# A decode kernel with more kept V, slots given out while the plan is made, and PSUM banks shared out differently

## The chip, the cores and the metric

The kernel runs on one core of a Trainium2 chip. The metric is the device time of one execution in microseconds; the median of several executions is quoted. The engines are PE (TensorE, the matrix engine, with its weight loads listed apart as PEld), DVE (VectorE), ACT (ScalarE), POOL (GpSimd) and SP, which here only issues transfers. SBUF is the on-chip memory with 128 partitions, PSUM the memory into which PE writes its sums; this kernel divides it into eight banks. "The stream" below is the flow of K and V from the chip's memory into SBUF.

## The reference

Two kinds of layer alternate, A, B, A, B, for eight rows of one token each:

```python
def _A_ref(x, k_cache, v_cache, wq, wo):          # 16 query heads, 8 KV heads, 4096 keys of 256
    q = ... x @ wq ...
    scores = jnp.einsum("bhqd,bhkd->bhqk", q, k) * (Dh ** -0.5)
    p = _softmax(scores, axis=-1)
    o = jnp.einsum("bhqk,bhkd->bhqd", p, v)
    return o... @ wo
def _B_ref(x, w1, w2, w3, w4): ...                # per token; with one token it is an MLP, w3 and w4
x = x + _A_ref(_layernorm(x), K, V, wq, wo)       # layer one
x = x + _B_ref(_layernorm(x), ...)
x = x + _A_ref(_layernorm(x), K, V, wq, wo)       # layer two: the same K and V
x = x + _B_ref(_layernorm(x), ...)
```

K and V of one row and head are 2 MB each. Both attention layers read the same caches, so what of a row stays in SBUF between its two layers need not be read again.

## The kernel before

Python code makes a list of operations with their dependencies, a scheduler orders them on each engine by modelled durations, and the engines get fixed instruction streams with semaphore waits. SBUF holds 30 slots for "quarters" (a quarter of one head's K or V, 128 partitions x 4096 bytes, 0.524 MB). Of each row, five K heads (20 quarters) and two V quarters are kept from layer one to layer two; 8 slots then carry the stream.

```python
KEEP_K = 5
KEEP_V = 2
...
def grab(n):                      # at program-building time, before anything is scheduled
    rank = {q: k for k, q in enumerate(free_slots)}
    for k, margin in ((4, MARGIN4), (2, MARGIN2), (1, 0)):
        ...                       # a run of 4, 2 or 1 slots, those freed longest ago first
...
# front(): K of a head. transposes of K pieces, then scores into the one score bank
wr=[("sc", par, x) ...], banks=["S"]
plan.op("dve", lambda v: v.tensor_reduce(pm, sview, ...), ..., banks=["S"])   # max, from PSUM
plan.op("act", ex, ..., banks=["S"])                                          # two exps, from PSUM
...
# back(): V of a head. weighted sum into the one bank psP, two evictions, row sums
par, no = 0, g % NO
ps, bk = psP, "P"
last = t.matmul(ps[g4:g4 + 2, PV0:PV0 + DH], pT[nr][:, i, :], slot_ap(q, s * 256, 256), ...)
plan.op("dve", lambda v: v.tensor_copy(oS[:, 0, :], po), ...)
plan.op("dve", lambda v: v.tensor_tensor(oS[:, 1, :], po, oS[:, 0, :], ALU.subtract), ...)
...
bank, bk2 = ROWS[layer]           # one bank for the row sums of each layer, four row groups
last = t.matmul(bank[32 * i:32 * i + 1, 0:D], oT[no][...], wo_sb[:, a:a + D], ...)
```

While row b's MLP (a chain of small operations, with the stream's kept slots occupied) runs between its two layers, the V of three heads of row b+1 keeps the stream busy. The last row, 7, has no next row; there an MLP over the other seven rows is done too.

## Time and profile before

| | before |
|---|---|
| median of 3 executions | 1143.41 us (1142.17 to 1145.31) |
| profiled span | 1139.0 us |
| loads | 455.19 MB in 376 cache loads and the weights |
| load queue, share of 16 engines' span | 97.3% |
| PE, PEld, DVE | 85%, 68%, 48% |
| granted PE clock | 0.932 |

How to read it: the transfers are busy nearly always, so the bytes set the time. The list of issues tells how they are cut (lines of the first page: tensor, count, KB of each, median us from issue to landing):

```profile
kv<-in_A_v_cache_dram SPq DMA_DIRECT2D x57, 2048.0 KB, 16.5
kv<-in_A_k_cache_dram SPq DMA_DIRECT2D x55, 2048.0 KB, 23.4
...
kv<-in_A_v_cache_dram SPq DMA_DIRECT2D x128, 512.0 KB, 11.3
```

A quarter takes 1.24 us at 424 GB/s, so the 11.3 us from issue to landing are at most nine quarters' worth, less what a load needs to start flowing (about 2 us, by the prediction's estimate): seven or eight quarters were in the queue when it was issued. That fits 8 slots all in flight at the MLPs: the slots, not the issue, seem to bound how far ahead the stream can be.

### The profile page before, as it was taken

The page shows a single profiled execution, that of the slowest core. Times are in us where ns is not written, and L with a number is a line of the kernel's source. Part 1 is how long each engine was busy: PE and PEld are TensorE (multiplying, and loading weights), DVE is VectorE, ACT ScalarE, POOL GpSimd, SP SyncE. Part 2 cuts the span into 40 slices and gives each one's busy share as a digit, 9 for nine tenths or more (in the row PEclk, how much of TensorE's full clock was granted, in tenths as well). Part 3 has the DMA queues.
Part 4 walks back from the last instruction along what each step waited for, and adds up shares of the span by engine and source line. Part 5 has one row for each costly group of instructions (what it writes and reads, how often), then busy time and mean ns, then how long its engine had stood idle before and what let it go on. Part 6 is the DMA issues. An engine that isn't in the chain of part 4 may idle for free.

```text
span 1139.0 us, 42316 instructions
## 1 busy us (share of the span) xinstructions
PE 967.5 (85%) x19513; PEld 775.8 (68%) x19513; DVE 541.1 (48%) x1630; ACT 259.8 (23%) x826; POOL 97.6 (9%) x273
## 2 busy tenths in 40 slices
PE   5788888898789987998888987989868998898887
PEld 4677566685668756886667855777557875676675
DVE  3344434554255543565445643555425554354453
ACT  1133112340123301232022410233012330232120
POOL 0000010010100100010010100011010010010010
PEclk9999899998899988899999988999899899999897
DMA  9999999999999999999999999999999999999992
GB/s 334 408 423 394 411 409 424 421 415 376 422 423 420 415 385 424 425 417 413 399 423 424 414 408 399 423 421 417 386 422 424 419 414 398 424 416 412 361 410 108
DMA packets 58705, 457.89 MB, mean 402 GB/s; under 512 B 6288, under 2 KB 9504, under 8 KB 26400
## 3 DMA queue, kind: packets, MB, share of 16 engines
q1 hardware_dynamic: 58528, 455.19, 97.3%
q8 instruction: 153, 2.51, 0.9%
q14 instruction: 24, 0.20, 0.0%
HBM read 455.16 MB, written 0.01 MB: 400 GB/s over the span
## 4 chain that ended last, share of the span: by engine, by line
DMA 45%; PE 43%; DVE 4%; issue 4%; SPq 3%; ACT 0%; POOL 0%
DMA kv<-in_A_k_cache_dram 23%; DMA kv<-in_A_v_cache_dram 22%; PE psT L985 14%; PE psS L836 12%; PE psP L887 7%; SPq L480 3%; PE psT L1153 2%; PE psM L692 2%; PE psR L934 2%; PE psM L789 1%; DVE oS L901 1%; DVE oS L899 1%; PE psM L708 1%; PE psM L792 1%; PE psP L909 1%
## 5 line engine op out<-in xcount | busy, mean ns | idle before, releaser
L985 PE MATMUL psT<-ident_f,kv 128*128 128x128 f32 x2816 | 389.5, 289 | 36.8 <-DMA kv<-in_A_k_cache_dram 31.9
L985 PEld LDWEIGHTS psT<-ident_f,kv 128*128 128x128 f32 x2816 | 322.8, 147 | 66.9 <-DMA kv<-in_A_k_cache_dram 42.6
L993 DVE COPY kv<-psT 128x512 f32<-128x512 f32 x401 | 273.9, 691 | 189.3 <-PE psT L985 181.8
L994 ACT COPY kv<-psT 128x512 f32<-128x512 f32 x303 | 177.8, 587 | 405.3 <-PE psT L985 401.1
L887 PE MATMUL psP<-kv,pT 128*2 128x256 bf16 x4096 | 164.4, 286 | 32.3 <-DMA kv<-in_A_v_cache_dram 18.6
L857 ACT ACTIVATE pT<-psS,nb 128x32 bf16<-128x32 f32 x256 | 75.3, 300 | 351.8 <-DVE nb L851 351.8
L836 PE MATMUL psS<-q2T,kv 128*128 128x48 bf16 x4096 | 134.2, 187 | 20.4 <-issue 18.3
L836 PEld LDWEIGHTS psS<-q2T,kv 128*128 128x128 bf16 x4096 | 122.4, 99 | 37.7 <-issue 32.2
L887 PEld LDWEIGHTS psP<-kv,pT 128*2 128x2 bf16 x4096 | 81.9, 84 | 72.4 <-issue 27.6
L836 PEld LDWEIGHTS psS<-q1T,kv 128*128 128x128 bf16 x4096 | 123.0, 97 | 9.7 <-issue 5.3
L836 PE MATMUL psS<-q1T,kv 128*128 128x48 bf16 x4096 | 128.9, 184 | 0.0
L849 POOL PARTITION_ALL_REDUCE gm<-pm x128 | 45.4, 355 | 775.5 <-DVE pm L847 775.5
L847 DVE TENSOR_REDUCE pm<-psS 128x2 f32<-128x64 f32 x128 | 28.7, 224 | 148.5 <-PE psS L836 146.5
L899 DVE CAST oS<-psP 128x256 bf16<-128x256 f32 x128 | 54.2, 423 | 63.5 <-PE psP L887 59.7
L1153 PE MATMUL psT<-ident_b 128*128 128x512 bf16 x220 | 75.3, 426 | 0.0
L862 POOL PARTITION_ALL_REDUCE Db<-rs x128 | 51.0, 398 | 229.5 <-ACT pT L857 229.5
L909 PEld LDWEIGHTS psP<-sel,oS 128*128 128x128 bf16 x512 | 25.7, 100 | 62.2 <-DVE oS L901 59.6
L909 PE MATMUL psP<-sel,oS 128*128 128x2 bf16 x512 | 32.2, 167 | 37.3 <-DVE oS L901 36.6
L901 DVE TENSOR_TENSOR oS<-psP,oS 128x256 bf16<-128x256 f32 x128 | 54.2, 424 | 3.2
L857 ACT ACTIVATION_READ_ACCUMULATOR pT<-psS,nb 128x1 f32 x256 | 50.9, 199 | 0.0
L934 PE MATMUL psR<-wo_sb,oT 128*1 128x448 bf16 x448 | 42.5, 368 | 6.2 <-DVE oT L915 3.0
L692 PE MATMUL psM<-x2c,wq_sb 128*128 128x24 bf16 x768 | 36.9, 184 | 9.0 <-issue 7.1
(121 smaller groups left out, 475.8 us busy)
## 6 DMA issues: line engine op xcount, KB each, us to landing
kv<-in_A_v_cache_dram SPq DMA_DIRECT2D x57, 2048.0 KB, 16.5
kv<-in_A_k_cache_dram SPq DMA_DIRECT2D x55, 2048.0 KB, 23.4
kv<-in_A_v_cache_dram SPq DMA_DIRECT2D x70, 1024.0 KB, 14.0
kv<-in_A_k_cache_dram SPq DMA_DIRECT2D x66, 1024.0 KB, 20.1
kv<-in_A_v_cache_dram SPq DMA_DIRECT2D x128, 512.0 KB, 11.3
wo_sb<-in_A_wo_dram SPq DMA_DIRECT2D x1, 3584.0 KB, 46.4
wq_sb<-in_A_wq_dram SPq DMA_DIRECT2D x3, 1024.0 KB, 17.0
w_sb<-in_B_w_dram SPq DMA_DIRECT2D x3, 448.0 KB, 22.8
```

The costliest lines, as they stand in the source:

```text
L692: last = t.matmul(bank[:, at + i * step:at + i * step + copies], w, r, start=(kc == 0), stop=(kc == 3))
L836: last = t.matmul(ps[:, 2 * i:2 * i + 2 * REP], a[:, c:256:2], bcast(rhs(c), REP, 1), start=(c == 0), stop=(c == 1))
L857: return a.activation(pT[nr][:, :, :].rearrange("p i j -> p j i")[:, jj, :], sview[:, jj, :], ACT.Exp, bias=nb[nm][:, jj:jj + 1], scale=IN ...
L887: last = t.matmul(ps[g4:g4 + 2, PV0:PV0 + DH], pT[nr][:, i, :], slot_ap(q, s * 256, 256), start=(i < 4), stop=(i >= 28), skip_group_check= ...
L899: plan.op("dve", lambda v: v.tensor_copy(oS[:, 0, :], po), 0.36, "o", rd=[("pv", par, x) for x in range(4)], wr=["oS0"], banks=[bk], prio=hi)
L901: plan.op("dve", lambda v: v.tensor_tensor(oS[:, 1, :], po, oS[:, 0, :], ALU.subtract), 0.36, "o", rd=["oS0"] + [("pv", par, x) for x in r ...
L909: last = t.matmul(ps[:, PV1 + 2 * c:PV1 + 2 * c + 2], oS[:, w, c:DH:2], sel[:, :], start=(w == 0), stop=(w == 1))
L934: last = t.matmul(bank[32 * i:32 * i + 1, 0:D], oT[no][:, i % 2, i // 2:i // 2 + 1], wo_sb[:, a:a + D], start=(k == 1), stop=(k == HKV - 1 ...
L985: last = t.transpose(psT[bank][:, s * P:(s + 1) * P], src, ident_f[:, :])
L993: return e.tensor_copy(dst, psT[bank][:, :])
L994: return e.copy(dst, psT[bank][:, :])
L1153: return t.matmul(psT[bank][:, :], ident_b[:, :], bcast(ident_b[:, :], 4, 1), start=True, stop=True)
```

## The change

Its intent: keep one V quarter more, and make seven working slots do what eight did. Slots are no longer fixed in program order but given out by the scheduler when its own clock says that a load could start, in runs of one to four. PSUM's eight banks are shared out anew: two banks for weighted sums (used in turn), paid for by putting both layers' row sums into one bank. The scores are copied to SBUF at once, so the score bank is free earlier. In the last row all queries come first and the seven-row MLP comes after three tasks.

The diff below leaves out smaller edits: the softmax has two sets of buffers in place of three, the scheduler counts 3.5 us from the issue of a load to its start in place of 2.4, and layer two's heads run as one list in place of two. The two MARGIN constants stand in the diff, but nothing in the changed kernel reads them.

```diff
-KEEP_V = 2
-MARGIN4, MARGIN2 = 16, 8
+KEEP_V = 3
+MARGIN4, MARGIN2 = 6, 2
+MLP_AT = 3
 ...
+    def next_kv(i):                       # in the scheduler, at each step
+        m = ...                           # up to 4 neighbouring quarters of one head, same fate
+        late = max(free["sp"], dma_end - self.LEAD)
+        ...                               # first time at which m neighbouring slots are free,
+        ...                               # or, if that is later than `late`, a shorter run
+        return t, m, q
 ...
-    psP = nc.alloc_psum_tensor("psP", [P, 512], f32)
-    psR = [nc.alloc_psum_tensor(f"psR{i}", [P, 512], f32) for i in range(2)]
+    psP = [nc.alloc_psum_tensor(f"psP{i}", [P, 512], f32) for i in range(2)]
+    psR = nc.alloc_psum_tensor("psR", [P, 512], f32)
 ...
+        plan.op("dve", lambda v: v.tensor_copy(ss[:, :], ps[:, 0:64]), 0.17, "max", rd=scs,
+                wr=[("sS", nm)], banks=[bk], prio=hi)      # max and exps then read ss
 ...
-        par, no = 0, g % NO
-        ps, bk = psP, "P"
+        par = g % 2
+        ps, bk = psP[par], f"P{par}"
 ...
-                    last = t.matmul(bank[32 * i:32 * i + 1, 0:D], ...
+                    r = 64 * layer + 32 * (i % 2)
+                    last = t.matmul(psR[r:r + 1, 0:D], ...   # two row groups a layer, not four
 ...
+            k = both(1, b, l2_heads, [(1, b, h) for h in free_heads])   # last row
+            run(k[:MLP_AT])
             mlp(x3T[:, :, :], "x3all", B, xoT[:, :, :], ["xo"])         # was after all of k
```

## The prediction

> **What bounds the kernel now.** I read the first page from the top: totals, the 40 slices, the queue and its issues.
>
> ```profile
> span 1139.0 us, 42316 instructions
> PE 967.5 (85%) x19513; PEld 775.8 (68%) x19513; DVE 541.1 (48%) x1630; ACT 259.8 (23%) x826; POOL 97.6 (9%) x273
> ...
> DMA  9999999999999999999999999999999999999992
> GB/s 334 408 423 394 411 409 424 421 415 376 422 423 420 415 385 424 425 417 413 399 423 424 414 408 399 423 421 417 386 422 424 419 414 398 424 416 412 361 410 108
> ...
> q1 hardware_dynamic: 58528, 455.19, 97.3%
> ```
>
> The transfers are at nine tenths or more in 39 of 40 slices, and the load queue's packets fill 97.3% of sixteen engines' span. PE at 85% looks close, but this count contains 220 filler matmuls (75.3 us) whose only purpose is the clock, and pipelined matmuls overlap in it. So the kernel is bound by the stream of K and V, and I ask only three things: how many bytes, in what packets, and where the stream stops.
>
> The stream's full rate comes from cutting the run into stretches. First a stretch of 2 MB loads (16 KB packets), then one of 512 KB loads (4 KB packets), then the stretch of the single-row MLP between layers, in pieces of 2 us:
>
> ```profile
> 200.00:220.00 20.00, 16.93 (x285) 14.37 (x284) 9.91 (x23) 5.79 (x17) 1.51 (x4) 1.00 1.01 426
> 258.00:264.00 6.00, 4.36 (x83) 2.52 (x81) 2.22 (x8) 1.43 (x6) 0.75 (x2) 1.00 1.02 412
> ...
> 276.00:278.00 2.00, 2.00 (x70) 1.93 (x67) 0.00 (x0) 0.00 (x0) 0.00 (x0) 0.96 0.97 385
> 278.00:280.00 2.00, 2.00 (x40) 1.23 (x42) 0.56 (x3) 0.00 (x0) 0.00 (x0) 0.50 0.53 211
> 280.00:282.00 2.00, 1.93 (x35) 0.91 (x23) 1.45 (x8) 0.00 (x0) 0.00 (x0) 0.69 0.91 236
> ```
>
> The last column is GB/s. 426 with 16 KB packets, 412 with 4 KB packets, and a dip to 211 while the MLP runs. Doing the same for every microsecond of the run, and counting what each microsecond below 340 GB/s lost against 424, gives this budget: start 5.4 us; seven MLP dips near 143, 272-282, 413, 548, 683, 819 and 954 us, 9.2 us together; one at 99 us, 0.9; 1059 to 1083 us, 3.9; the end from 1117 us, 21.2.
>
> Why the dip? The timeline of VectorE and PE there:
>
> ```profile
> 272.96 0.61 PE L887 MATMUL psP<-kv,pT 128*2 128x256 bf16 x16
> ...
> 274.19 0.41 DVE L899 CAST oS<-psP 128x256 bf16<-128x256 f32 x1
> 274.63 0.42 DVE L901 TENSOR_TENSOR oS<-psP,oS 128x256 bf16<-128x256 f32 x1
> ...
> 278.32 1.02 PE L887 MATMUL psP<-kv,pT 128*2 128x256 bf16 x16
> ```
>
> A head's weighted sum ends at 273.5 us, its eviction waits behind the MLP's small VectorE operations until 274.19, and the next head's first matmul into the same bank comes only at 278.32. For almost 5 us no V slot comes free, and the queue runs dry.
>
> The end, from the chain that ended last:
>
> ```profile
> 1115.55 1.81 PE psP L887 x27
> ...
> 1120.21 1.32 PE psP L887 x29
> 1121.55 0.43 DVE oS L899
> ...
> 1123.36 0.90 PE psP L887 x32
> 1124.29 0.44 DVE oS L899
> ...
> 1127.80 0.43 DVE oS L901
> ```
>
> The last bytes land near 1118 us (344 GB/s in 1115-1118, 35 in the next 3 us). By then PE has just left the seven-row MLP (its second matmul block starts at 1113) and still owes several heads, each waiting for the one bank. The last eviction starts at 1127.43; from there to the end is 11.6 us of serial work.
>
> **What the Trainium skill says.** (1) "DMA: Bandwidth & Descriptors", section Specifications: a fabric ceiling of 435 GB/s, and about 358 GB/s from HBM for one core. The trace agrees with the first and not the second: 426 is held for 20 us, so there is no faster rate left to gain and bytes are time. (2) "Perfetto Trace Analysis", section Identifying the Most-Contended Engine: matmul busy share is no measure of nearness to the limit, and the weight-load share is better; here 68% against DMA 97.3%, which agrees with my choice. (3) The same page, Matmuls: independent groups should rotate through PSUM banks, so that an eviction overlaps the next group. The 5 us hole above is what it looks like when they do not. (4) "PSUM — Partial Sum Buffer", section The four PSUM rules: a start flag clears accumulation state over the bank and the 32-partition quadrants written. The two layers' row sums go to rows 0 and 32, and 64 and 96, so they may share a bank; no run so far shows it.
>
> **The change part by part.**
>
> *Third kept V quarter.* A quarter is 128 partitions x 4096 bytes = 0.524 MB. One more kept for each of 8 rows saves 8 x 0.524 = 4.19 MB of 455.19; at 424 GB/s that is **-9.9 us**, all of it on the path. The built instruction stream confirms it: 488 V quarters issued in place of 496, K unchanged at 352.
>
> *Runs of one to four, given out by the plan's clock.* The cache loads go from 376 to 389: 121 of 2 MB (before 112), 22 of 1.5 MB (none), 44 of 1 MB (136), 202 of 512 KB (128). Each load is 128 packets, so 13 x 128 = 1664 packets more. The two rates give the price of a packet: on one engine 16 KB take 16384/(426/16) = 615 ns, four of 4 KB 4 x 4096/(412/16) = 636 ns, so three extra packets cost 21 ns, 7 ns each. 1664 x 7 / 16 engines = **+0.7 us**. The stretches that are full already cannot get fuller by a better choice of slot.
>
> *Two banks for the weighted sums against one slot less.* At an MLP, 20 K quarters and 2 V quarters are held, and 8 slots of 30 carry the stream; after, 7. One slot is 0.524/424 = 1.24 us of stream. What hides the MLP is 12 V quarters of three heads plus the free slots: before 20 x 1.24 = 24.7 us, after 19 x 1.24 = 23.5 us. The need: from the last V of the layer (265.3 us) to the first freed K slots (284.3 to 286.4, when the first scores end) is 19 to 21 us, plus about 2 us from issue to flow (my estimate: the first loads are issued from 0.73 us on, and the first 4 us move 104 GB/s on average, 1 us' worth of full stream, so it flows from 3 us): 21 to 23 us. So 7 slots are just enough if V is used promptly, which the second bank allows. I take a third of the 9.2 us back: **-3 us**, with room either way.
>
> *Copy of the scores out of PSUM.* 128 copies of 128x64, at about the 0.22 us of the reduction over the same elements = 28 us more VectorE, from 48% to about 50%. It lies beside the stream. It frees the score bank some 2 us earlier per head (now held until the second exponential), useful right after an MLP. **0 us** taken by itself.
>
> *One bank for both layers' row sums, a memset and constants.* It pays for the second bank. Same 448 matmuls; row sums now go one after another into two row groups instead of four. 368 ns x 4 per head is all there is, beside the stream. **0 us.**
>
> *The order.* The head order of layer two stays (kept K first). The first load after a kept-K stretch now comes one task earlier. For the last row all queries are made at once and the seven-row MLP is put after three tasks, not after all of them. This takes it off PE's end. In the built order the last heads' weighted sums alternate banks with nothing but filler and row sums between, so PE should be waiting for DMA there. Then the end is one last quarter's 8 matmuls (0.3), eviction to finish 11.6 us as above, and up to 1.3 us for the row-sum evictions that share VectorE: 13 to 14 us after the last byte in place of 20.8. **-6.5 us.** Of the 3.9 us lost at 1059-1083 I take back **0.5**.
>
> Sum: -9.9 + 0.7 - 3 - 6.5 - 0.5 = -19.2 us; 1143.4 - 19.2 = 1124.2. I round up to **1125**, since two of the terms are hopes and the first is arithmetic.
>
> **The rivals.**
> (A) *Bytes saved, holes widened.* The load queue already waits most for scores, and each MLP has one slot less. If each of seven dips loses the full 1.24 us more, and the banks bring nothing, 8.7 us are given back, and with the end gained the time is 1143.4 - 9.9 + 0.7 + 8.7 - 7 = 1136. For it:
>
> ```profile
> SPq L480 <- PE psS L836: 533.2, 96, 20.1
> SPq L480 <- PE psP L887: 315.7, 140, 9.4
> ```
>
> These are slot waits, though, with the queue mostly still full behind them; by themselves they show no loss. Against it: the seen hole is a V hole, not a K one.
> (B) *Everything lines up.* All dips closed and the end at 13 us: 1143.4 - 9.9 + 0.7 - 9.2 - 7.8 - 3 = 1114. Against it: seven slots leave under 1.5 us of slack by my own count.
> (C) *The plan's clock is wrong.* Slots are now chosen by simulated times; where the chip is later, a load waits at the head of the in-order queue for one slot while another stands empty. Or the fewer fillers (166 against 220) leave PE at a lower clock (granted 0.932 on average now). Either could cost several us across the run and end near 1140.
>
> **Range and chances.** Bytes and packets (-9.2) are nearly sure: 1134 with nothing else. The end's -6.5 is likely, the dips may go -9 to +9. Hence 1125, 8 in 10 between 1114 and 1137. Faster by over 2% means below 1120.5, a gain of 22.9: it needs most of the dips closed too, 0.29. Slower by 2% needs a new stall of over 30 us, 0.02. Within 2%: 0.69.
>
> **What would show it.** The queue should move 451.0 MB in about 60,200 packets. Stretches of 2 MB loads should still read 426. Seven dips of under 1 us each confirm the banks; dips of 2.5 us confirm (A), with the queue waiting for scores. From the last byte to the end should be 13 to 14 us. The weighted sum of the next head should start before the eviction of the last one is over. The prediction is wrong if the end stays near 20 us (then PE, not the order, set it), if the full-rate stretches fall below 420, or if new holes appear outside the MLPs, which would be (C).

## The result and the profile after

The changed kernel took 1132.31 us (median of 4, 1130.72 to 1132.89); the kernel before 1144.36 (4 runs in all, 1142.17 to 1147.04). The ratio is 0.9891, 95% interval 0.9867 to 0.9916. A ratio here and below is the mean time of one kernel's runs over that of the other's of the same rounds, so not quite the ratio of the medians. Executions over 1.5% slower than the fastest of the same kernel are left out of the means. It is a real gain of 1.1%, inside the range, and within 2%.

The lines of the first page that answer to those of before:

```profile
span 1131.1 us, 42368 instructions
PE 971.4 (86%) x19459; PEld 776.7 (69%) x19459; DVE 552.0 (49%) x1742; ACT 279.8 (25%) x846; POOL 98.0 (9%) x273
...
GB/s 331 409 424 420 391 414 424 423 413 384 418 424 426 414 381 420 426 423 412 380 426 423 424 400 400 423 424 421 372 413 424 423 418 384 424 422 393 378 376 121
...
q1 hardware_dynamic: 60400, 450.99, 97.7%
...
kv<-in_A_v_cache_dram SPq DMA_DIRECT2D x183, 512.0 KB, 8.7
```

The bytes fell by the 4.2 MB that were kept; the packets rose; the full slices still read 424 to 426. The 512 KB loads now land 8.7 us after their issue. That would fit a shorter queue, but they are no longer the same loads (183 in place of 128), so it is not shown. The slices with the six MLPs between 200 and 1010 us (384, 381, 380, 400, 372, 384) are no better than before (376, 385, 399, 399, 386, 398), and those ahead of the last one read 393, 378, 376 where before they read 412, 361, 410.

There is an exact account of this. Cut the run into microseconds and count for each what it is short of 424 GB/s; then the span is the moved bytes at 424 plus the sum of these losses. Before: 457.89/0.424 + 59.1 = 1139.0. After: 453.70/0.424 + 61.0 = 1131.1. So between these two executions the bytes gave **-9.9 us**, and everything else together **+1.9 us**. They are single executions, and that of the kernel before was a quick one (1140.88 us against a median of 1144.36). By the times of all runs (the mean of two ratios, below) the change gained 12.2 us, 2.3 more than its bytes. So everything else was worth somewhere between 2 us lost and 2 us gained, where the prediction had summed 9.3 us gained. This is where its missing 7 us are.

Did the second bank do what it was for? The timeline of PE and DVE at the same MLP of the changed kernel, with idle time and its releaser in brackets:

```profile
270.28 0.61 PE L970 MATMUL psP<-kv,pT 128*2 128x256 bf16 x16
...
271.48 0.42 DVE L982 CAST oS<-psP 128x256 bf16<-128x256 f32 x1
271.93 0.42 DVE L984 TENSOR_TENSOR oS<-psP,oS 128x256 bf16<-128x256 f32 x1
...
271.88 0.61 PE L970 MATMUL psP<-kv,pT 128*2 128x256 bf16 x16 [0.66 <-DMA kv<-in_A_v_cache_dram]
...
277.89 0.39 PE L970 MATMUL psP<-kv,pT 128*2 128x256 bf16 x8 [0.89 <-DMA kv<-in_A_v_cache_dram]
```

The next head's sum starts at 271.88, while the eviction of the last one is still going on, so that step was right. But where PE waits now, it is for V that has not landed. The hole was not closed, it changed hands. The stretches of 2 us there, last column GB/s:

```profile
270.00:272.00 2.00, 1.34 (x39) 0.74 (x39) 1.83 (x11) 0.00 (x0) 0.00 (x0) 1.00 0.92 332
272.00:274.00 2.00, 2.00 (x44) 0.95 (x37) 0.68 (x4) 0.21 (x1) 0.00 (x0) 1.00 0.90 322
...
278.00:280.00 2.00, 1.75 (x39) 0.87 (x33) 0.91 (x7) 0.00 (x0) 0.00 (x0) 0.93 0.95 315
280.00:282.00 2.00, 2.00 (x17) 0.51 (x14) 1.24 (x5) 0.00 (x0) 0.00 (x0) 0.50 0.95 313
```

One deep dip (211, 236) became two shallow ones of about the same area. Over the whole stretch from 200 to 1010 us, with six MLPs, the loss was 20.4 us before and 22.0 after. Not all of this is in the dips: microseconds under 340 GB/s, the prediction's own measure of a dip, lost 8.4 us of it before and 8.9 after.

The end, in stretches of 3 us (us, PE, PEld, DVE, ACT, POOL busy with counts, clock, DMA share, GB/s):

```profile
1089.00:1092.00 3.00, 3.00 (x61) 2.97 (x60) 2.49 (x5) 1.26 (x6) 0.40 (x1) 1.00 0.85 280
1092.00:1095.00 3.00, 3.00 (x108) 2.43 (x105) 1.58 (x6) 0.60 (x2) 0.36 (x1) 1.00 0.85 306
1095.00:1098.00 3.00, 3.00 (x49) 2.32 (x44) 1.20 (x6) 1.98 (x8) 0.76 (x2) 1.00 0.95 322
...
1107.00:1110.00 3.00, 1.58 (x31) 0.79 (x35) 1.53 (x6) 0.67 (x4) 0.35 (x1) 0.86 0.98 411
1110.00:1113.00 3.00, 3.00 (x64) 1.92 (x65) 0.29 (x2) 0.06 (x1) 0.40 (x1) 0.57 0.30 117
1113.00:1116.00 3.00, 2.42 (x63) 1.58 (x58) 1.80 (x6) 0.00 (x0) 0.00 (x0) 1.00 0.00 0
```

The stream's rate falls away at 1111 us and the kernel ends at 1131.1: 20 us, as before, not 13 to 14. (The last load has landed only at 1113.3, 17.7 us before the end; where the text below says that the stream ends, it means the fall of the rate below 100 GB/s.) PE is full at 1089 to 1098 while the stream falls to 280, and it still has weighted sums to do after the last byte. The chain that ended last says how many:

```profile
1107.43 0.32 PE psS L915 x6
...
1110.74 2.11 PE psP L970 x41
...
1117.27 0.35 PE psP L970 x8
```

The last score ends only at 1107.75, and its weights come after a softmax; from 1107.7 to 1117.6 PE runs the weighted sums of 18 quarters (144 matmuls), about 13 of them after the stream's end at 1111. So the reading of the end in the prediction ("PE should be waiting for DMA there") failed.

### The profile page after: what moved, and what is told of

Its sections match the earlier page's. It is cut to its first block, busy times and chain, and to the rows that moved or that the text cites. A ratio compares the mean times of both kernels' runs of the same rounds, so it can differ in the third digit from the quotient of the medians.

```text
span 1131.1 us, 42368 instructions
## 1 busy us (share of the span) xinstructions
PE 971.4 (86%) x19459; PEld 776.7 (69%) x19459; DVE 552.0 (49%) x1742; ACT 279.8 (25%) x846; POOL 98.0 (9%) x273
## 2 busy tenths in 40 slices
DMA packets 60578, 453.70 MB, mean 401 GB/s; under 512 B 6496, under 2 KB 9712, under 8 KB 36080
## 3 DMA queue, kind: packets, MB, share of 16 engines
q1 hardware_dynamic: 60400, 450.99, 97.7%
## 4 chain that ended last, share of the span: by engine, by line
PE 51%; DMA 38%; issue 6%; DVE 4%; POOL 0%; ACT 0%; SPq 0%; POOLq 0%
DMA kv<-in_A_k_cache_dram 28%; PE psT L1067 19%; PE psS L915 14%; DMA kv<-in_A_v_cache_dram 8%; PE psP L970 8%; PE psR L1017 3%; PE psM L771 2%; PE psT L1231 1%; DMA w_sb<-in_B_w_dram 1%; DVE oS L982 1%; PE psM L868 1%; DVE oS L984 1%; PE psP L992 1%; PE psM L871 1%; ACT pT L940 0%
## 5 line engine op out<-in xcount | busy, mean ns | idle before, releaser
L1075 DVE COPY kv<-psT 128x512 f32<-128x512 f32 x381 | 262.4, 691 | 214.3 <-PE psT L1067 213.4
L1067 PEld LDWEIGHTS psT<-ident_f,kv 128*128 128x128 f32 x2816 | 321.8, 147 | 48.8 <-DMA kv<-in_A_k_cache_dram 29.7
L970 PE MATMUL psP<-kv,pT 128*2 128x256 bf16 x4096 | 175.6, 286 | 16.3 <-DMA kv<-in_A_v_cache_dram 8.4
L940 ACT ACTIVATE pT<-sS,nb 128x32 bf16<-128x32 f32 x256 | 81.8, 326 | 345.8 <-DVE nb L934 345.8
L915 PEld LDWEIGHTS psS<-q1T,kv 128*128 128x128 bf16 x4096 | 138.9, 98 | 13.7 <-issue 9.5
L915 PE MATMUL psS<-q1T,kv 128*128 128x48 bf16 x4096 | 146.1, 184 | 2.2 <-issue 2.0
L927 DVE COPY sS<-psS 128x64 f32<-128x64 f32 x128 | 28.7, 224 | 124.7 <-PE psS L915 120.1
L1017 PE MATMUL psR<-wo_sb,oT 128*1 128x448 bf16 x448 | 67.3, 382 | 10.0 <-DVE oT L998 6.4
L1231 PE MATMUL psT<-ident_b 128*128 128x512 bf16 x166 | 57.0, 418 | 0.0
L940 ACT ACTIVATION_READ_ACCUMULATOR pT<-sS,nb 128x1 f32 x256 | 48.1, 188 | 0.0
L771 PEld LDWEIGHTS psM<-x2c,wq_sb 128*128 128x128 bf16 x768 | 30.2, 99 | 24.5 <-issue 19.6
```

The lines of the kernel that those rows point to most:

```text
L771: last = t.matmul(bank[:, at + i * step:at + i * step + copies], w, r, start=(kc == 0), stop=(kc == 3))
L915: last = t.matmul(ps[:, 2 * i:2 * i + 2 * REP], a[:, c:256:2], bcast(rhs(c), REP, 1), start=(c == 0), stop=(c == 1))
L940: return a.activation(pT[nr][:, :, :].rearrange("p i j -> p j i")[:, jj, :], sview[:, jj, :], ACT.Exp, bias=nb[nm][:, jj:jj + 1], scale=IN ...
L1017: last = t.matmul(psR[r:r + 1, 0:D], oT[no][:, i % 2, i // 2:i // 2 + 1], wo_sb[:, a:a + D], start=(k == 1 and i < 2), stop=(k == HKV - 1 ...
L1067: last = t.transpose(psT[bank][:, s * P:(s + 1) * P], src, ident_f[:, :])
L1075: return e.tensor_copy(dst, psT[bank][:, :])
```

## The experiments

Two questions were open: what the parts are worth, since their sum was nearly the bytes alone; and what holds the end. Twelve runs were made, the last of them the changed kernel again, each timed in five rounds beside the kernel before. An interval on a ratio is about plus or minus 0.0025. The change itself was run twice, 0.9891 and 0.9895, mean 0.9893; "against the change" below is the difference of a ratio to this mean times 1144 us, good to about 3.4 us (both intervals together). "Lost" is the account above, from one profiled execution each; the two executions of the change itself differ by up to 3 us in a column. A profiled execution also need not be a typical one: against its kernel's median it was 3.5 us quicker for the kernel before and 3.7 for the old banks, 2.6 us slower for the change again and 3.9 for four quarters kept. The column of 200 to 1010 us is called "the MLP stretch" below.

| run | ratio to before | against the change, us | lost 200-1010 us | lost 1010 us to the end |
|---|---|---|---|---|
| before | 1 | +12.2 | 20.4 | 27.5 |
| the change | 0.9891 | | 22.0 | 28.7 |
| the change again | 0.9895 | | 24.9 | 27.6 |
| two V quarters kept | 0.9959 | +7.6 | 22.3 | 24.5 |
| before, three kept | 1.0044 | +17.3 | 32.5 | 28.9 |
| old banks | 1.0027 | +15.3 | 31.4 | 29.5 |
| seven-row MLP last | 0.9929 | +4.1 | 23.7 | 29.0 |
| less PE work at the end (wrong result) | 0.9848 | -5.1 | 24.4 | 20.9 |
| four V quarters kept | 0.9913 | +2.3 | 29.7 | 33.8 |
| one weighted-sum bank | 1.0018 | +14.3 | 31.1 | 30.9 |
| scores left in PSUM | 0.9939 | +5.3 | 26.6 | 28.9 |
| fixed slots | 1.0010 | +13.4 | 25.3 | 33.7 |
| wide seven-row MLP | 0.9918 | +2.9 | 23.3 | 31.8 |
| early keys | 0.9915 | +2.5 | 23.1 | 30.2 |

### Two V quarters kept, all else changed

```diff
-KEEP_V = 3
+KEEP_V = 2
```

> The changed kernel with two V quarters kept again, so 8 slots carry the stream at each MLP and 455.2 MB are read. Theory 1 (bytes are time, the slot costs nothing because the second bank keeps V moving): slower than the changed kernel by 9 to 10 us, about 1142 us. Theory 2 (the ninth-tenth of that is lost again because 7 slots widen the MLP dips): slower by only 1 to 4 us, about 1134 to 1136 us, with 1 us less loss per dip than the changed kernel.

It took 1138.61 us (ratio 0.9959, interval 0.9934 to 0.9985), 7.6 us more than the change. The arithmetic of the bytes, 9 to 10, lies inside the error, 1 to 4 just outside. And the eighth slot did not make the loss in the MLP stretch smaller (22.3 against 22.0 and 24.9). So theory 1 fits better: with the rest of the change in place the slot's cost, 2.3 us give or take 3.4, cannot be told from nothing.

### The kernel before with three V quarters

```diff
-KEEP_V = 2
+KEEP_V = 3        # in the kernel before
```

> The kernel before with three V quarters kept and nothing else: one weighted-sum bank, slots fixed in program order. Theory 1 (bytes alone): 9 to 10 us faster than before, about 1134 us, the same as the whole change, and then the rest of the change was worth about 2 us. Theory 2 (the fixed slots and the one bank cannot bear 7 slots): gains under 5 us, 1139 or more, with MLP dips of 2 us or more each, and the allocator and banks were what made the third quarter pay.

It took 1147.5 us, 1.0044 (1.0019 to 1.0068): slower than before with 4.19 MB less to read. Neither theory had gone that far; the second was nearest. The MLP stretch lost 32.5 us in place of 20.4, 2 us more at each MLP, more than the slot's 1.24. The third quarter alone is a loss, and the rest of the change is worth 17 us once it is kept, but only about 5 us (0.9959 against 1) with two kept. The parts are not terms of a sum.

### Old banks, and one weighted-sum bank

```diff
-    psP = [... for i in range(2)];  psR = ...          # two sum banks, one row-sum bank
+    psP = [...("psP0", ...)] * 2;   psRs = [... for i in range(2)]
-        par = g % 2
+        par = 0
-                    r = 64 * layer + 32 * (i % 2)
+                    r = 32 * i                          # four row groups again
```

> The changed kernel with the PSUM banks of before: one bank for weighted sums, one per layer for the row sums with four row groups. Theory 1 (the second bank closes part of the MLP dips): slower than the changed kernel by 3 to 8 us, each dip 0.5 to 1 us larger. Theory 2 (the second bank's gain is paid back because two row groups make the row sums run one after another on PE): within 2 us, row sums back at 42 us of PE instead of 67.

The second kernel took only the alternation away and left the row sums in their shared bank:

```diff
-        par = g % 2
+        par = 0
```

> The changed kernel with every weighted sum in one bank, and the row sums still in two row groups of one bank. Theory 1 (the 15 us of the run with the old banks came from the weighted sums alone): as slow as that run, 1144 to 1149 us, MLP dips as large. Theory 2 (row sums in two groups also cost): another 2 us or more slower than that run.

They took 1146.83 us (1.0027, 1.0002 to 1.0051) and 1145.71 us (1.0018, 0.9992 to 1.0045), the same within error. So the second bank for weighted sums is worth about 15 us with seven slots (with eight no run tried it), where the prediction had 3 for bank and slot together, and the row sums cost nothing visible: with four row groups their PE time fell from 67.3 to 43.6 us and no time came with it. The loss is in the dips: microseconds under 340 GB/s in the MLP stretch lost 21 us in both runs, against 8.9 and 10.4 in the two executions of the change. The deep dip is back in the run with the old banks:

```profile
276.00:278.00 2.00, 2.00 (x42) 1.19 (x43) 0.57 (x4) 0.00 (x0) 0.00 (x0) 0.53 0.59 199
278.00:280.00 2.00, 2.00 (x35) 0.96 (x23) 1.41 (x7) 0.00 (x0) 0.00 (x0) 0.62 0.86 233
```

The granted clock (the column before the last two) reads 0.53 and 0.62 here and read 0.50 in the dip of the kernel before. It is not what makes the dip: with one weighted-sum bank alone the same four microseconds read 188 and 252 GB/s at a clock of 1.00.

As for correctness, two layers' open sums share a bank in different groups of 32 partitions in every run of the change, and each agreed with the reference. That is support, not proof: one run below agrees too although its scores are wrong.

### The scores left in PSUM

```diff
-        plan.op("dve", lambda v: v.tensor_copy(ss[:, :], ps[:, 0:64]), ...)
-        sview = ss[:, :].rearrange("p (i j) -> p j i", j=2)
+        sview = ps[:, 0:64].rearrange("p (i j) -> p j i", j=2)   # max and exps hold the score bank
```

> The changed kernel without the copy of the scores to SBUF: maximum and exponentials read the score bank, as before. Theory 1 (as predicted, the copy is worth nothing by itself): within 1.5 us of the changed kernel. Theory 2 (scores of kept heads free K slots sooner after an MLP, which 7 slots need): 3 us or more slower, with larger dips at 280, 415 and so on, the queue waiting for scores.

It took 1136.61 us, 0.9939 (0.9916 to 0.9962), 5.3 us more than the change. That is theory 2's size: an additional DVE operation per head, 28.7 us of DVE in all, saves time. That it does so by letting go of the bank is argued, not shown: the account has 26.6 us in the MLP stretch against 22.0 and 24.9, and the load queue did not wait longer for scores, as theory 2 had it (352.5 us against 507.0), but for weighted sums (505.3 against 372.2).

### Fixed slots

The allocator of before was put back into the changed kernel, with its margins and its 2.4 us from issue to start.

```diff
-    o.frees = ks[u]                        # slots given out by the scheduler's clock
+    free_slots.append(ks[u])               # and taken by grab() in program order
```

> The changed kernel with slots fixed in program order as before (loads of 1, 2 and 4 quarters, 377 cache loads in place of 389), everything else of the change kept. Theory 1 (the prediction's: the choice of slot is worth nothing but its 0.7 us of extra packets): within 2 us of the changed kernel, about 1131 to 1134 us. Theory 2 (with 7 slots, a load that waits for its own slot while another stands empty costs stream): slower by 4 us or more, with dips 0.5 us or more larger each. Theory 3 (the plan's clock is wrong often enough to hurt): faster by 3 us or more; the sum of the other parts measured alone, larger than the whole, would fit that.

It took 1145.1 us, 1.0010 (0.9985 to 1.0035), 13.4 us more. Theory 2 in size, but not in place: the MLP stretch lost 25.3, hardly more than with the change (22.0 and 24.9); 6.6 us were lost between 30 and 200 us (the change: 4.1), and 12.4 between 1010 and 1095 us (the change: 7.7). There one load waited for its own slot (the queue's waits and its issues in that stretch):

```profile
SPq L571 <- PE psS L935: 26.0, 6, 11.2
...
1067.96 2.03 SPq L571 DMA_DIRECT2D kv<-in_A_v_cache_dram  x2
1081.56 0.33 SPq L571 DMA_DIRECT2D kv<-in_A_k_cache_dram  x1
```

One wait of 11.2 us for scores, and nothing issued between 1070 and 1081.5 us. A long wait alone proves little: the change has one of 12.9 us for scores between 1010 and 1095 us. That the free choice of slots would have filled just this wait is possible, but the two kernels also order PE's work differently, so it is argued, not shown.

### Four V quarters

```diff
-KEEP_V = 3
+KEEP_V = 4
```

> The changed kernel with all four V quarters of the last head kept, 6 slots at each MLP, another 4.19 MB less. Theory 1 (with the second bank a slot costs little: two kept against three was 7.7 us slower): 5 to 8 us faster than the changed kernel, about 1126 us. Theory 2 (7 slots were just enough by the prediction's count, so 6 are too few, and each of seven dips loses another 1.2 us): within 2 us of the changed kernel, with dips 1 us or more larger.

It took 1133.87 us, 0.9913 (0.9885 to 0.9941), no better than the change with another 4.2 MB less. The MLP stretch lost 29.7 us, about 1 us more at each MLP, and the last row 5 us more (its profiled execution was its slowest, 1137.77 us). Theory 2: with this bank and slot machinery three quarters are where it turns.

### The end: seven-row MLP last

```diff
-MLP_AT = 3
+MLP_AT = 99       # after all tasks of the last row's kept heads, as before
```

> The changed kernel with the seven-row MLP after all tasks of the last row's kept heads, where it stood before. Theory 1 (moving it was to shorten the end, and does not): within 1.5 us of the changed kernel, 20 us from the last byte to the end in both. Theory 2 (it does help but something else took its place at the end): 3 us slower or more, with the end at 23 us or more.

It took 1135.02 us, 0.9929 (0.9907 to 0.9951), 4.1 us more than the change, just outside the error, and in its profile the stream ended 23 to 24 us before the kernel did. That is nearer to theory 2, that moving the MLP does help. But the account from 1010 us on shows nothing of it (29.0 against 28.7 and 27.6), so the size of the help is uncertain (4.1 us, give or take 3.4), and the predicted 6.5 us for the end are not seen there.

### The end: less PE work (wrong result)

```diff
-            if u in fresh:
+            if u in fresh and not (layer == 1 and b == B - 1):
                 for pc in range(2):
                     transpose_piece(ks[u], pc)
```

> The changed kernel without the transposes of the last row's three fresh K heads in layer two (24 pieces of 4 matmuls, about 0.45 us each, 11 us of PE, and their evictions). Wrong result on purpose; every load, slot and score stays. Theory 1 (at the end PE is behind the stream, the last weighted sums wait for PE): 5 to 8 us faster than the changed kernel, 13 to 15 us from the last byte to the end. Theory 2 (the end is a serial chain of softmax, evictions and MLP that starts when the bytes are there): under 2 us faster, the end stays near 20 us.

It took 1126.84 us, 0.9848 (0.9824 to 0.9872), 5.1 us less than the change. (The scores of three heads of one row are wrong; the comparison with the reference passed all the same, so it is not sensitive to them.) The account from 1010 us on falls from 28.7 to 20.9 us. The end of its chain:

```profile
1095.84 15.70 DMA kv<-in_A_v_cache_dram
...
1111.59 0.39 PE psP L970 x8
```

Now the chain comes straight from the last load, which lands at 1111.5, one quarter's 8 matmuls follow, and 14.0 us later (1125.5) the kernel ends: the chain that the prediction had described for the change. The 14.0 is not to be set against the 20 above: by the same measure, the landing of the last load, the change has 17.7 us in one execution and 14.9 in the other. It is the time and the sum from 1010 us on that fell. So the work on the last row's fresh keys, not the order of its last heads, holds the end. This is theory 1, at the lower edge of its range. The edit takes away the evictions of the transposes on DVE and ACT too; that it is PE which matters is read from the trace of the change, where PE is full from 1089 to 1098 us and DVE is not.

### The end: wider matmuls, and earlier keys

Two correct kernels tried to use this. In the first the seven-row MLP's moving side is repeated four times, because PE's granted clock reads 0.50 from 1080 to 1088 us, beside that MLP (the first of its two blocks of matmuls is shown; the second is widened likewise):

```diff
-            pe(lambda t: h_mms(t, lambda kc: yb[:, kc, :], ch, 0, B, B), 56,
+            pe(lambda t: h_mms(t, lambda kc: bcast(yb[:, kc, :], 4, 1), ch, 0, 4 * B, 4 * B), 56,
```

> The changed kernel with the moving side of the seven-row MLP's matmuls repeated four times (32 columns in place of 8, the first 8 used), same count of matmuls. Theory 1 (the granted clock of 0.5 at 1079 to 1088 us comes from those narrow matmuls, and PE is behind the stream at the end because of it): clock back to 0.9 or more in that stretch, the end shorter by 2 to 5 us. Theory 2 (the low clock has another cause, or PE catches up anyway): clock still near 0.5 there, or the end within 1 us of the changed kernel's.

It took 1135.0 us, 0.9918 (0.9891 to 0.9945), not faster than the change. Its clock:

```profile
1080.00:1082.00 2.00, 2.00 (x86) 2.00 (x82) 0.68 (x4) 0.73 (x4) 0.36 (x1) 1.00 0.99 328
1082.00:1084.00 2.00, 0.82 (x12) 0.25 (x8) 1.13 (x6) 0.30 (x1) 0.40 (x1) 1.00 1.02 377
1084.00:1086.00 2.00, 0.57 (x15) 0.57 (x15) 0.07 (x1) 0.00 (x0) 0.00 (x0) 0.78 1.02 393
1086.00:1088.00 2.00, 2.00 (x65) 1.96 (x63) 0.00 (x0) 0.00 (x0) 0.00 (x0) 0.50 1.02 395
```

The clock is 1.00 at 1080 to 1082 us and falls to 0.50 only after PE had been idle for most of 1082 to 1086. So the low clock is not the mark of the narrow matmuls, as theory 1 had it; here it followed idle time. The unedited change's second execution shows the same: its narrow block at 1079 to 1081 us runs at 1.00, PE is idle for most of 1082 to 1085, and from 1085 to 1094 us the clock is 0.50. Whether the low clock helps to put PE behind stays open, since this run did not raise it: in the change twelve transposes take 2.35 us at 0.50 (from 1086.95) and 1.51 at 1.00 (from 1099.47).

In the second the last row's three fresh K heads come one to two tasks earlier:

```diff
-            k = both(1, b, l2_heads, [(1, b, h) for h in free_heads])
+            k = both(1, b, l2_heads, [(1, b, h) for h in free_heads], at_=(-5, -5, -4))
-MLP_AT = 3
+MLP_AT = 4
```

> The changed kernel with the three fresh K heads of the last row loaded and scored one to two tasks earlier, ahead of that row's V loads (12 K quarters in a row, then V), and the seven-row MLP after the fourth task. Correct result. Theory 1 (the end is PE work, transposes and scores, that stands behind V that has landed): 2 to 6 us faster than the changed kernel, 13 to 16 us from the last byte to the end. Theory 2 (the same PE work only moves the hole: it is spared at the end and lost in the stream around 1040 to 1090 us): within 2 us, with more than 8 us lost in that stretch.

It took 1134.72 us, 0.9915 (0.9894 to 0.9936). The stream ends some 17 us before the kernel does, and the stretch from 1010 to 1095 us lost 11.7 us, against 7.7 and 6.9 in the two executions of the change; from 1010 us to the end it is 30.2 against 28.7 and 27.6. That fits theory 2: the PE work can be moved, but the loss goes with it. No version that beats the change came out of these runs.

### The change again

The unedited changed kernel, as the measure.

> The changed kernel itself once more, unedited, as the measure for the runs that differ from it by a few microseconds. Theory: a ratio between 0.987 and 0.992 again; the end near 20 us and 7 to 8 us lost between 1010 and 1095 us again, if those are properties of the kernel and not of the one profiled execution.

1132.19 us, 0.9895 (0.9873 to 0.9917). In this execution the stream ended about 17 us before the end, not 20, and 4.7 us were lost at 1092 to 1103 us instead; the sum from 1010 us on is 27.6 against 28.7. So the split between "the end" and "the stretch before it" varies from run to run, and only the sum should be compared.

## Why the prediction was right, and where not

The range, the direction and "within 2%" were right; the middle, 1125, was 7 us too low. That the total came close to "1134 with nothing else" is in part luck: the third quarter alone was no gain of 9 us but a loss of 5, and the choice of slots, which the prediction valued at 0, was as necessary as the second bank to turn it into a gain (with either one taken away alone the time is 1145 us or more). Its steps:

- *The bound is the stream; bytes are time.* Right. The full stretches read 424 to 426 as before, and in the account of the two profiled spans the bytes are -9.9 us. The run with two quarters kept put 7.6 us, error 3.4, on the third one.
- *Packets, +0.7.* Of 60,400 packets, 1664 more are those computed, and 208 of under 512 bytes were not counted. The price came from a misread stretch: 258 to 264 us holds 405 packets of 4 KB and 97 of 8 KB, and not 4 KB alone. The traces' records of the packets have medians of 162 ns for 4 KB before and 159 after, and of 313 for 8 KB and 614 for 16 KB in both. That is an estimate of 7 to 12 ns for each further packet, so +0.7 to +1.2 us. No run measured it apart.
- *Two banks against one slot: "-3 us, with room either way".* **No such net gain is seen.** Under 340 GB/s the MLP stretch lost 8.9 and 10.4 us in the two executions of the change and 8.4 before; with one profile of the kernel before, a quick one, a small gain is not excluded. The mechanism was half right: the next head no longer waits for an eviction, but then it waits for V. And the 5 us hole of before was not all the bank's: the last reader of the bank was done at 275.57 us, and until 278.3 PE had row sums and the MLP's second block of matmuls to do before the next head. What the step overlooked is how much the missing slot costs with one bank: about 15 us (5.0 us slower with 9.9 us of bytes saved), not the 8.7 of rival (A). The bank, with the rest, paid for the slot, and little more. (By the prediction's own count the slack of seven slots is 0.5 to 2.5 us, not "under 1.5".)
- *Copy of the scores, 0, and choice of slots, 0 apart from packets.* Wrong as worths: taken away alone they cost 5.3 and 13.4 us. It did not hurt the total because they, too, only keep up what was there.
- *The end, "-6.5 us".* **This is the term that made the miss;** with the 0.5 beside it, it is as large as the miss. It came from the sentence that "PE should be waiting for DMA there". PE was behind the stream with three heads' transposes and scores. With the transposes gone the loss from 1010 us on fell to 20.9 us (the run with a wrong result); with them in place it did not move (27.5 before, 28.7 and 27.6 after). The prediction had named this sign itself: "wrong if the end stays near 20 us (then PE, not the order, set it)". The built order of instructions tells what follows what, not whether PE will be ahead or behind; that takes a sum of PE's work in the stretch against the stream's, which the prediction did not make.
- *Rival (C), the plan's clock is wrong.* Not seen: fixed slots were 13 us slower, and the mean clock stayed (0.933).

What stays open: why single removals (15.3, 13.4, 5.3 and 4.1 us) add up to far more than the 17.3 us that all of them together bring over the kernel before with three quarters; one reason may be that every removal makes the scheduler lay out the whole program anew (it put in 166 filler matmuls for the change, 195 with one weighted-sum bank, 186 with the scores left in PSUM, 204 with fixed slots), so that a run takes away more than its part; how much the low clock costs in the last row; and how much the moved MLP helps, which the times show at the edge of the error and the account does not show.

## What to carry to other kernels

When a kernel is bound by its stream of bytes, keeping more on chip pays by the bytes, but each kept buffer is taken from the stream's run-ahead; test the saving together with whatever lets the remaining buffers go sooner, since the saving alone can be a loss (here 5 us). A second bank or an early copy out of one can be worth many microseconds (here about 15 and 5) although the engine that empties it is half idle; the likely reason is that it decides when an input buffer is free. And before a gain is booked at the end of a kernel, add up the work that each engine owes in the last stretch: an order that looks right does not help an engine that is behind.

## What the Trainium skill lacked or had wrong

- "DMA: Bandwidth & Descriptors", section Specifications: the table gives about 358 GB/s from HBM for one core without a condition, and read so, as the prediction did, it did not hold: 426 GB/s was held for 20 us and 400 over the whole run. The page is not wrong: its section on measured bandwidth says further down that this share is for two cores streaming at once. The fabric ceiling of 435 agrees.
- No page gives a measured price of packets between 4 and 16 KB on the sync queue. The packet records of the kernels before and after have medians of 162 and 159 ns for 4 KB, and of 313 for 8 KB and 614 for 16 KB: an estimate of 7 to 12 ns for each further packet on an engine.
- "Perfetto Trace Analysis", section Identifying the Most-Contended Engine, judges TensorE by its weight-load share. Over the run it was 69%, and yet in 9 us of the last row PE was full (weight loads 7.72 of 9 us, at 1089 to 1098 us) while the stream fell to 280 to 322 GB/s: the share of the whole run did not show it, that of the stretch did. The page's measure holds; it is to be taken stretch by stretch.
